# Batches 4 to 7: the first half of the pooled products half a slot sooner, and one P product a slot sooner

## The chip, the cores and the metric

One core of one Trainium2 chip. The metric is the device time of one execution in microseconds (us); the time given for a kernel is the median of its runs. "Profile" and "trace" mean one execution recorded by the hardware profiler.

## The reference

An attention with 32 learned memory slots per head is followed by a two-layer network. For 8 batches, 8 heads, 576 positions and head size 64:

```
a      = softmax(phi)                   # over the 32 memories
k_m    = sum over s of a[s,m] * k[s]    # pooled keys
v_m    = sum over s of a[s,m] * v[s]    # pooled values
attn   = softmax(q @ k_m.T / 8)         # over the 32 memories
x      = attn @ v_m                     # 4608 tokens x 512
h      = x @ w_in                       # 512 x 2048
out    = (h - tanh(h)) @ w_out          # 2048 x 512
```

## The kernel before, in words

**What is computed where.** The tokens are cut into 18 units of 256 tokens, and the 2048 hidden columns into 4 blocks `fb`. Since x is never needed itself, the kernel first makes P = v_m @ w_in for each batch and block (`att_p`, L524, one product per block, called P{b}0 to P{b}3), and then h = attn @ P (`mm1`, L572). All large products run as two or three half-precision products of high and low parts, and h - tanh(h) is a cubic in three VectorE and ScalarE steps. `mm2_blocks` (L686 on; products at L702, L708 and L715) multiplies with w_out in a scheme of seven block products.

**Slots.** After a hand-written start (`START`), one loop runs over slots `sl` from 18 on, one for each unit u and block fb: sl = 4u + fb. In each slot TensorE's own work stands in a fixed order:

- `mm1` of this slot's unit and block, into the one PSUM tile hs; ScalarE squares it (L579) and VectorE goes on with it (L587, L597), ScalarE then rounds it (L603) and GpSimd makes its low part (L608);
- `do(0)`: the first group of this slot's tasks;
- `mm2_blocks` of the unit and block two slots back, into the PSUM tiles x and o;
- `do(1)`: the second group, issued before the rest of the elementwise work;
- after a unit's last block: `evict`, which reads x and o with VectorE (L768 to L780) and sends the result off;
- `do(2)`: the third group, at the slot's end.

**Tasks.** `PLAN` (batches 4 to 7) and `PLAN3` (batch 3) say at which slot, counted from the batch's first one, a task stands. In a string, what is ahead of `;` and `|` goes to `do(0)`, what follows `;` to `do(1)`, what follows `|` to `do(2)`. The first slots of batches 3 to 7 are 24, 36, 44, 52 and 60, so that slot -8 is slot 28, 36, 44 and 52 for batches 4, 5, 6 and 7, and slot -7 is the one after it. `in_order` fixes every engine's instructions in the order in which they are written: nothing is rescheduled, and an instruction that waits holds up all that stands behind it on its engine.

**The tasks the change touches, and their neighbours.**

- KR{b}0, KR{b}1 (`load_kv_half`, L126): keys and values of row half 0 or 1, in two DMAs of 516 KB each (heads 0 and 1, heads 2 and 3), issued by SyncE's queue (SPq). Both halves use the same ring of two buffers (tag "q"), so KR{b}1 can only start when the products on KR{b}0's data are done.
- X, XP, YM, YE (L146, L157, L162 and L168, L182): the softmax of phi. XP brings the maxima to PSUM, ScalarE copies them, GpSimd subtracts them (L162, and L168 twice), ScalarE takes the exponential (L182, tile e). XP and YM are the last tasks of slot -9; YE stands in slot -8, in `do(1)`.
- V{b}0, V{b}1 (`pool_half`, L220, and L228 for the tail): the pooled products of row half 0 or 1, 32 matmuls each with weights from e, and 16 more for the tail in V{b}1. Both write one PSUM tile, pkv. V{b}0 needs the exponential and KR{b}0, V{b}1 needs KR{b}1.
- N, QT, U, S: normalization of the pooled sums, load of q, transposition, scores.
- P{b}3 and PL{b}3 (L524; ScalarE L537; VectorE L542): the last P product of a batch with its two roundings. PSUM tile pp has the same one buffer as pkv and all of the attention's other products.

Of the kernel before, what the change touches and what calls it, by code (L numbers as in the profile page):

```python
# [18 lines left out]
P = 128  # L19
# [318 lines left out]
def split_path(ctx, tc, c, ins, out):  # L338
# [502 lines left out]
    for word in START.split():  # L841
# [5 lines left out]


    PLAN = (
# [5 lines left out]
    PLAN3 = (  # L855
# [3 lines left out]
    )  # L859

    PLAN_C = (
# [227 lines left out]
@with_exitstack  # L1089
def tile_kernel(ctx: ExitStack, tc: tile.TileContext, qt, kva, kvt, pha, phx, w_in, w_out, out):  # L1090
    nc = tc.nc
    ins = dict(qt=qt, kva=kva, kvt=kvt, pha=pha, phx=phx, w_in=w_in, w_out=w_out)
    const = ctx.enter_context(tc.tile_pool(name="const", bufs=1))
    c = {"first": len(nc.cur_bb.bb.instructions)}
    for name, shape, dt in (
        ("ident", [P, P], F32), ("ones", [P, P], F32), ("ones16", [P, 1], F16), ("one", [P, 1], F32),
        ("beta", [P, 1], F32), ("idw", [P, P], F32), ("nidp", [P, P], F16), ("idw", [P, P], F32), ("nid16", [P, P], F16), ("stat", [P, N_CHECK], F32), ("bad", [P, 1], I32),
    ):
        c[name] = const.tile(shape, dt, name=name)
    make_identity(nc, c["ident"])  # L1100
    nc.vector.tensor_scalar(c["nid16"], c["ident"], -1.0, None, op0=ALU.mult)
    nc.vector.tensor_scalar(c["nidp"], c["ident"], -S_V * S_W / S_P, None, op0=ALU.mult)
    nc.vector.tensor_scalar(c["idw"], c["ident"], S_W, None, op0=ALU.mult)
    nc.gpsimd.memset(c["ones"], 1.0)
    nc.gpsimd.memset(c["ones16"], 1.0)
    nc.gpsimd.memset(c["one"], 1.0)
    nc.gpsimd.memset(c["beta"], BETA)
    with ExitStack() as inner:
        split_path(inner, tc, c, ins, out)
    with tc.If(c["wide"] > 0):  # L1110
        with ExitStack() as inner:
            wide_path(inner, tc, c, ins, out)
# [39 lines left out]
```

## Time and profile before

| | |
|---|---|
| median of 3 runs | 660.62 us (660.04 to 660.83) |
| the profiled execution's own time | 660.87 us |
| its span | 659.1 us |
| PE (TensorE matmuls) busy | 641.5 us, 97% |
| DVE (VectorE) busy | 522.7 us, 79% |
| ACT (ScalarE) busy | 375.7 us, 57% |
| POOL (GpSimd) busy | 251.0 us, 38% |
| share of PE in the chain that ended last | 76% |
| TensorE clock granted | full speed over the run |

A timeline row has the start in us, the duration in us, the engine (PEld is TensorE's weight load, SPq is SyncE's queue of DMAs), the line in the kernel, operation, output and inputs, the count, and in brackets the idle time of the engine just before the row and what ended it; "issue" stands for idle time in which nothing that the profile shows was waited for. Rows of one kind that follow each other are merged. The chain view follows back from the last instruction what each piece of work had waited for.

### The profile page before, as it was taken

The page shows a single profiled execution, that of the slowest core. Times are in us where ns is not written, and L with a number is a line of the kernel's source. Part 1 is how long each engine was busy: PE and PEld are TensorE (multiplying, and loading weights), DVE is VectorE, ACT ScalarE, POOL GpSimd, SP SyncE. Part 2 cuts the span into 40 slices and gives each one's busy share as a digit, 9 for nine tenths or more (in the row PEclk, how much of TensorE's full clock was granted, in tenths as well). Part 3 has the DMA queues.
Part 4 walks back from the last instruction along what each step waited for, and adds up shares of the span by engine and source line. Part 5 has one row for each costly group of instructions (what it writes and reads, how often), then busy time and mean ns, then how long its engine had stood idle before and what let it go on. Part 6 is the DMA issues. An engine that isn't in the chain of part 4 may idle for free.

```text
span 659.1 us, 15599 instructions
## 1 busy us (share of the span) xinstructions
PE 641.5 (97%) x6690; PEld 455.5 (69%) x6690; DVE 522.7 (79%) x790; ACT 375.7 (57%) x509; POOL 251.0 (38%) x173
## 2 busy tenths in 40 slices
PE   8879999999999999999999999999999999999996
PEld 4355656566557777777776777777687777887785
DVE  6989999999855787875988679767977686867763
ACT  4567686666424456545655465545654577666541
POOL 0315141221222245442535253625452455455521
PEclk9999999999999999999999999999999999999999
DMA  8999245302423402333331524141505333234201
GB/s 342 375 377 393 96 169 184 114 2 65 145 96 102 145 20 74 113 101 133 105 114 65 168 66 153 60 142 66 163 25 195 101 100 125 61 109 142 77 33 37
DMA packets 25996, 84.98 MB, mean 129 GB/s; under 512 B 2880, under 2 KB 2880, under 8 KB 25152
## 3 DMA queue, kind: packets, MB, share of 16 engines
q1 hardware_dynamic: 24624, 81.55, 36.1%
q10 hardware_dynamic: 1296, 2.36, 0.9%
q8 instruction: 54, 0.88, 0.6%
q14 instruction: 22, 0.18, 0.1%
HBM read 72.37 MB, written 11.53 MB: 127 GB/s over the span
## 4 chain that ended last, share of the span: by engine, by line
PE 76%; DVE 12%; DMA 6%; issue 2%; ACT 2%; POOL 1%; SPq 0%; DVEq 0%; ACTq 0%
PE hs L572 20%; PE x L715 13%; PE o L708 12%; PE o L715 10%; PE o L651 6%; PE h L572 4%; DMA kv<-in_kva_dram 3%; PE o1h L651 3%; PE pp L524 3%; PE pkv L220 2%; DMA raw<-in_w_out_dram 2%; DVE h L587 2%; DVE wt L384 1%; DVE h L597 1%; PE psc L272 1%
## 5 line engine op out<-in xcount | busy, mean ns | idle before, releaser
L608 POOL TENSOR_TENSOR g<-h,g 128x1024 f16<-128x1024 f32 x64 | 138.5, 2165 | 329.2 <-ACT g L603 234.3
L572 PEld LDWEIGHTS <-ph 128*128 128x128 f16 x2304 | 176.7, 98 | 20.7 <-issue 6.0
L572 PE MATMUL hs<-ah,ph 128*128 128x256 f16 (+3 forms) x1152 | 151.5, 246 | 0.0
L587 DVE SCALAR_TENSOR_TENSOR h<-hs,u 128x1024 f32<-128x1024 f32 x54 | 65.9, 1220 | 91.3 <-ACT u L579 91.2
L603 ACT ACTIVATE g<-h 128x1024 f16<-128x1024 f32 x72 | 75.9, 1055 | 91.7 <-DVE h L597 89.5
L572 PE MATMUL hs<-al,ph 128*128 128x256 f16 (+3 forms) x576 | 127.6, 246 | 0.0
L592 ACT ACTIVATE u<-u,beta 128x1024 f32<-128x1024 f32 x72 | 82.4, 1147 | 55.1 <-DVE h L587 54.1
L708 PE MATMUL o<-wout_hi,g 128*128 128x512 f16 x432 | 104.7, 380 | 0.0
L715 PEld LDWEIGHTS <-f 128*128 128x128 f16 x896 | 87.5, 98 | 10.3
L597 DVE SCALAR_TENSOR_TENSOR h<-u,h 128x1024 f32<-128x1024 f32 x72 | 87.4, 1216 | 0.8 <-ACT u L592 0.7
L579 ACT ACTIVATE u<-hs 128x1024 f32<-128x1024 f32 x54 | 55.0, 1019 | 55.3 <-PE hs L572 50.8
L715 PE MATMUL x<-bt,f 128*128 128x256 f16 x672 | 82.5, 273 | 0.0
L715 PEld LDWEIGHTS <-g 128*128 128x128 f16 x672 | 64.1, 98 | 26.6 <-issue 5.0
L708 PEld LDWEIGHTS <-g 128*128 128x128 f16 x432 | 40.5, 98 | 44.0 <-issue 8.1
L651 PEld LDWEIGHTS <-g 128*128 128x128 f16 x384 | 36.6, 98 | 46.6 <-issue 3.4
L621 DVE TENSOR_TENSOR f<-g 128x512 f16<-128x512 f16 x112 | 64.9, 620 | 4.3 <-POOL g L608 3.4
L651 PE MATMUL o<-wout_hi,g 128*128 128x512 f16 x192 | 58.8, 380 | 0.0
L572 PE MATMUL h<-ah,ph 128*128 128x256 f16 (+3 forms) x384 | 49.6, 246 | 0.1
L572 PE MATMUL h<-al,ph 128*128 128x256 f16 (+2 forms) x192 | 42.4, 246 | 0.2 <-POOL al L515 0.2
L542 DVE SCALAR_TENSOR_TENSOR ph<-pp,ph 128x1024 f16<-128x1024 f32 x31 | 37.6, 1213 | 0.6 <-ACT ph L537 0.6
L537 ACT ACTIVATE ph<-pp 128x1024 f16<-128x1024 f32 x32 | 32.5, 1017 | 7.4 <-PE pp L524 7.4
L651 PE MATMUL o<-wout_lo,g 128*128 128x512 f16 x96 | 36.4, 379 | 0.0
(146 smaller groups left out, 979.1 us busy)
## 6 DMA issues: line engine op xcount, KB each, us to landing
kv<-in_kva_dram SPq DMA_DIRECT2D x20, 516.0 KB, 4.2
q<-in_qt_dram SPq DMA_DIRECT2D x16, 576.0 KB, 4.3
chk<-in_w_in_dram SPq DMA_DIRECT2D x16, 512.0 KB, 5.6
chk<-in_w_out_dram SPq DMA_DIRECT2D x16, 512.0 KB, 3.4
out_dram<-r SPq DMA_DIRECT2D x27, 256.0 KB, 2.4
kv<-in_kva_dram SPq DMA_DIRECT2D x6, 1032.0 KB, 9.0
raws<-in_w_in_dram SPq DMA_DIRECT2D x12, 512.0 KB, 7.2
raw<-in_w_out_dram SPq DMA_DIRECT2D x12, 512.0 KB, 6.6
```

Of the source, the lines that this page charges most:

```text
L542: nc.vector.scalar_tensor_tensor(pl, pa, S_P / (S_V * S_W), ph, op0=ALU.mult, op1=ALU.subtract)
L572: nc.tensor.matmul(hp[:, k, tu : tu + w], px[:, g, cs], d[ax][:, g, ta : ta + w], start=(n == 0), stop=(n == 5),)
L579: nc.scalar.activation(uu, hp, AF.Square, scale=1.0 / (S_A * S_P))
L587: nc.vector.scalar_tensor_tensor(h3, hp, C2 * S_G / (S_A * S_P), uu, op0=ALU.mult, op1=ALU.mult)
L592: nc.scalar.activation(uu, uu, AF.Square, bias=c["beta"])
L597: nc.vector.scalar_tensor_tensor(h3, uu, CC, hp, op0=ALU.add, op1=ALU.mult)
L603: nc.scalar.activation(gg[:, 0], h3, AF.Copy)
L608: eng.tensor_tensor(gg[:, 1], h3, gg[:, 0], op=ALU.subtract)
L621: nc.vector.tensor_tensor(o, x, y, op=op)
L651: nc.tensor.matmul(o, gx[:, k, P * tt : P * tt + P], wx[:, 4 * fb + k, :], start=(first and k == 0 and wx is wout_hi and gx is gh), stop=( ...
L708: nc.tensor.matmul(o[th], gg[:, 0, k, P * th : P * th + P], wout_hi[:, 4 * fb + k, :], start=(first and k == 0), stop=False)
L715: nc.tensor.matmul(dst, a(1 - n, kk), b(n, kk), start=(new and kk == 0 and n == 0), stop=(end and kk == 1 and n == 1))
```

## The change

Two tables change, and nothing else. In `PLAN`, V{b}0 goes from the head of slot -7 (`do(0)`, behind `mm1`) to the end of slot -8 (`do(2)`), for batches 4 to 7. KR{b}1 keeps its place at the head of slot -7, where it now is the first task. In `PLAN3`, P33 and PL33 go from slot 26 to slot 25, ahead of batch 3's AE31 and AD31.

```
-  (-8, "; YE{0}"), (-7, "V{0}0 KR{0}1 | V{0}1 N{0} QT{0}0"),
+  (-8, "; YE{0} | V{0}0"), (-7, "KR{0}1 | V{0}1 N{0} QT{0}0"),
...
-  (1, "; AE{0}1 | AD{0}1"), (2, "P{0}3 PL{0}3 ; AT{0}1"),
+  (1, "P{0}3 PL{0}3 ; AE{0}1 | AD{0}1"), (2, "; AT{0}1"),
```

On TensorE, around slots 36 and 37 (batch 5). Names: o and x are tiles of `mm2_blocks`, hs that of `mm1`, pkv that of V50 (weights e, data kv). Before, V50 stands behind the last product of slot 37's `mm1`:

```order
L572 LDWEIGHTS ph_4407
L572 MATMUL hs<-ah_4378,ph_4407 128x256
L220 MATMUL pkv_4603<-kv_4341,e_4166 32x129 [waits DMAHW5_49,DVE_49,Activation_49]
L220 MATMUL pkv_4603<-kv_4341,e_4166 32x129
L220 MATMUL pkv_4603<-kv_4343,e_4166 32x129 [waits DMAHW6_49]
...
L715 LDWEIGHTS g_4453
L715 MATMUL x<-wout_hi,g_4453 128x256
```

Now it stands between the last product of slot 36's `mm2_blocks` and the first of slot 37's `mm1`:

```order
L715 LDWEIGHTS f_4411
L715 MATMUL o_4297<-wout_lo,f_4411 128x256
L220 MATMUL pkv_4575<-kv_4341,e_4166 32x129 [waits DMAHW5_49,DVE_49,Activation_49]
L220 MATMUL pkv_4575<-kv_4341,e_4166 32x129
L220 MATMUL pkv_4575<-kv_4343,e_4166 32x129 [waits DMAHW6_49]
...
L572 LDWEIGHTS ph_4407
L572 MATMUL hs<-ah_4378,ph_4407 128x256
```

V50 has moved ahead of 24 matmuls of `mm1`; its wait for ScalarE (the exponential) has moved with it. SyncE's order is what it was.

On VectorE, slots 25 and 26 (ph is the tile of PL33, f the block forms that `mm2_blocks` uses a slot later, x and o what `evict` reads):

```order
 L587 SCALAR_TENSOR_TENSOR h_3318<-hs,u_3316 128x1024
+L542 SCALAR_TENSOR_TENSOR ph_3345<-pp_3320,ph_3345 128x1024
...
-L780 SCALAR_TENSOR_TENSOR r_3332<-o_2967,r_3332 128x512
...
-L587 SCALAR_TENSOR_TENSOR h_3439<-hs,u_3437 128x1024
-L542 SCALAR_TENSOR_TENSOR ph_3466<-pp_3441,ph_3466 128x1024
...
+L780 SCALAR_TENSOR_TENSOR r_3360<-o_2967,r_3360 128x512
```

PL33 (L542) now stands ahead of slot 25's `evict` instead of behind it; on TensorE the 48 instructions of P33 move from behind slot 26's `mm1` to behind slot 25's.

4 rows, old and new, of tables (PLAN, PLAN3) are left out of this document.

## The prediction

> **What bounds the kernel now.** First the page: the span, and the engine that fills it.
>
> ```profile
> span 659.1 us, 15599 instructions
> PE 641.5 (97%) x6690; PEld 455.5 (69%) x6690; DVE 522.7 (79%) x790; ACT 375.7 (57%) x509; POOL 251.0 (38%) x173
> ```
>
> Since start and end of a span are a case of their own, I next asked for the busy time of the stretch that the slot loop fills (columns: stretch, its length, then busy time and instructions of PE, PEld, DVE, ACT, POOL, then the granted clock, the DMA share and GB/s):
>
> ```profile
> 192.00:606.00 414.00, 411.88 (x4556) 313.00 (x4554) 318.00 (x483) 237.90 (x321) 183.16 (x119) 1.00 0.32 104
> ```
>
> In these 414 us PE is idle for 414.00 - 411.88 = 2.12 us. So PE sets the pace: work on other engines is paid for only where PE has to wait for it, any new wait of PE is paid in full, and no change of order alone can win much more than 2 us here. What little idle time there is, the waits of PE name (total, times, longest, in us), and the chain shows the place; these are its rows around batch 5's V50 and V51:
>
> ```profile
> PE pkv L220 <- DMA kv<-in_kva_dram: 2.5, 3, 1.0
> ```
>
> ```profile
> 351.16 2.62 PE hs L572 x24
> ...
> 355.25 5.54 DMA kv<-in_kva_dram
> 360.79 0.04 issue
> 360.83 1.08 PE pkv L220 x28
> ```
>
> The chain leaves PE for one DMA: V51, the second half of the pooled products, waits for the load KR51. That load had to wait for V50, which frees its buffers. This is the wait that the change can remove. But V50 itself has a supplier, the exponential on ACT, and what matters most below is when that ends. I took the timeline of all four places: for each, the weight loads of `mm1` (their start is where `mm2_blocks` has ended and where V0 will now stand), the exponential L182, V0 and V1. Batch 4, slots 28 and 29:
>
> ```profile
> 283.50 2.61 PEld L572 LDWEIGHTS <-ph 128*128 128x128 f16 x24
> 283.86 1.17 ACT L182 ACTIVATE e<-e 128x1152 f32<-128x1152 f32 x1 [1.30 <-POOL e L168]
> 286.32 0.82 PEld L220 LDWEIGHTS pkv<-kv,e 128*32 128x32 f32 x32 [0.21 <-issue]
> ...
> 292.24 0.97 PEld L220 LDWEIGHTS pkv<-kv,e 128*32 128x32 f32 x32 [0.21 <-issue]
> 293.41 0.18 PEld L228 LDWEIGHTS pkv<-kt,e 64*32 64x32 f32 x16 [0.20 <-issue]
> ```
>
> Batch 5, slots 36 and 37, with the GpSimd work ahead of the exponential:
>
> ```profile
> 347.89 2.36 POOL L162 TENSOR_TENSOR e<-e,ms 128x1024 f32<-128x1024 f32 x1
> 350.20 1.24 POOL L168 TENSOR_TENSOR e<-e,ms 64x128 f32<-64x128 f32 x2
> 350.88 2.61 PEld L572 LDWEIGHTS <-ph 128*128 128x128 f16 x24
> 351.48 1.17 ACT L182 ACTIVATE e<-e 128x1152 f32<-128x1152 f32 x1 [1.85 <-POOL e L168]
> 353.70 0.82 PEld L220 LDWEIGHTS pkv<-kv,e 128*32 128x32 f32 x32 [0.21 <-issue]
> 354.73 0.33 PEld L715 LDWEIGHTS <-g 128*128 128x128 f16 x4 [0.20 <-issue]
> 354.83 0.81 SPq L126 DMA_DIRECT2D kv<-in_kva_dram  x2
> 359.62 0.14 PEld L220 LDWEIGHTS pkv<-kv,e 128*32 128x32 f32 x4 [0.21 <-issue]
> 360.83 0.81 PEld L220 LDWEIGHTS pkv<-kv,e 128*32 128x32 f32 x28 [1.07 <-DMA kv<-in_kva_dram]
> 361.84 0.18 PEld L228 LDWEIGHTS pkv<-kt,e 64*32 64x32 f32 x16 [0.20 <-issue]
> ```
>
> Batch 6, slots 44 and 45:
>
> ```profile
> 420.25 2.72 PEld L572 LDWEIGHTS <-ph 128*128 128x128 f16 x48
> 420.79 1.17 ACT L182 ACTIVATE e<-e 128x1152 f32<-128x1152 f32 x1 [1.79 <-POOL e L168]
> 429.05 0.14 PEld L220 LDWEIGHTS pkv<-kv,e 128*32 128x32 f32 x4 [0.21 <-issue]
> 430.47 0.18 PEld L228 LDWEIGHTS pkv<-kt,e 64*32 64x32 f32 x16 [0.20 <-issue]
> ```
>
> Batch 7, slots 52 and 53:
>
> ```profile
> 489.00 2.77 PEld L572 LDWEIGHTS <-ph 128*128 128x128 f16 x48
> 489.54 1.16 ACT L182 ACTIVATE e<-e 128x1152 f32<-128x1152 f32 x1 [1.79 <-POOL e L168]
> 493.42 1.22 DVE L587 SCALAR_TENSOR_TENSOR h<-hs,u 128x1024 f32<-128x1024 f32 x1 [0.86 <-ACT u L579]
> 497.79 0.14 PEld L220 LDWEIGHTS pkv<-kv,e 128*32 128x32 f32 x4 [0.21 <-issue]
> 498.86 0.81 PEld L220 LDWEIGHTS pkv<-kv,e 128*32 128x32 f32 x28 [0.92 <-DMA kv<-in_kva_dram]
> 499.87 0.18 PEld L228 LDWEIGHTS pkv<-kt,e 64*32 64x32 f32 x16 [0.20 <-issue]
> 500.25 0.84 PEld L572 LDWEIGHTS <-ph 128*128 128x128 f16 x15 [0.20 <-issue]
> ```
>
> In each of the four the exponential starts only after PE has come to the end of slot -8. Today `mm1`, 2.6 to 2.8 us of work, stands between the two and covers it. The change takes that cover away.
>
> **Part 1: the wait that is removed.** Without a wait, V1 takes 293.41 - 292.24 = 1.17 us up to its tail (batch 4). In batches 5, 6 and 7 it takes 361.84 - 359.62 = 2.22, 430.47 - 429.05 = 1.42 and 499.87 - 497.79 = 2.08 us: waits of 1.05, 0.25 and 0.91, together 2.21 us. Do they go? In batch 5 the loads are issued 354.83 - 353.70 = 1.13 us after V50's start, and V51 can go on 360.83 - 353.70 = 7.13 us after it. In the new order, from V50's start to V51's stand V50 (354.73 - 353.70 = 1.03), `mm1` (353.70 - 350.88 = 2.82) and `mm2_blocks` (359.62 - 354.73 = 4.89): 8.74 us. The data is there 1.6 us early, so the whole 2.21 is won. SyncE's queue has the same order as before, so nothing new stands ahead of these loads or is held up behind them for longer. Bounds: 0 won, if the loads take 1.6 + 1.05 us longer, and 2.5 us, the total of the waits view.
>
> **Part 2: the wait that is added.** V0 would start 0.21 us (the issue gap before V0 in batches 4 and 5) after the last weight load of `mm2_blocks`, but the exponential ends later, and 0.04 us (the chain's issue piece between the DMA and V51) go by until PE moves:
>
> - batch 4: 283.86 + 1.17 + 0.04 = 285.07, against 283.50 + 0.21 = 283.71: 1.36 us
> - batch 5: 351.48 + 1.17 + 0.04 = 352.69, against 351.09: 1.60 us
> - batch 6: 420.79 + 1.17 + 0.04 = 422.00, against 420.46: 1.54 us
> - batch 7: 489.54 + 1.16 + 0.04 = 490.74, against 489.21: 1.53 us
>
> Together 6.03 us. What is queued behind V0 on PE is the next slot's `mm1`. Can that run meanwhile? Batch 7 shows it: while V71 waits for its data until 498.86, the `mm1` behind it, whose tile hs is free since VectorE read it (493.42 + 1.22 = 494.64), starts to load weights only at 500.25, after V71. The wait is not filled.
>
> The Trainium skill (TensorE: Matmul & The Clock Gate, Part 2) says why: "The MATMULs themselves stay in program order"; only weight loads are pulled ahead. By that rule this part costs the whole 6.03 us; were matmuls taken out of order it would cost nothing. The trace agrees with the rule.
>
> Nor does the pause bring the exponential forward. It stands behind GpSimd's subtractions, which run without a break from 347.89 to 350.20 + 1.24 = 351.44 in batch 5, 0.04 us before ACT starts; all of it descends from earlier slots that the change leaves alone. Bounds: at the low end the signal costs nothing and the issue gap behind V0 (0.20, as behind V1) is gone, 4 x 0.24 less, 5.1; at the high end the wait brings one more such gap, 4 x 0.20 more, 6.8. I take 6.0, straight from the rows.
>
> The other engines then get slot -7's `mm1` 2.4 to 2.6 us later (the wait and V0), but in the chain rows above they are not on the path, and PE's next use of what they make is a slot or two later.
>
> **Part 3: P33.** PE does the same work, sooner. VectorE gets PL33 ahead of slot 25's `evict`, and slot 26's `mm2_blocks` may write x and o only when `evict` has read them; today P33 stands between. The rows of slot 26 (VectorE's reads L769 and L780, PE's first writes of x and o, PL33):
>
> ```profile
> 261.44 0.42 DVE L769 SCALAR_TENSOR_TENSOR r<-x,r 128x256 f32<-128x256 f32 x1
> 262.45 1.28 DVE L780 SCALAR_TENSOR_TENSOR r<-o,r 128x512 f32<-128x512 f32 x2
> 263.52 0.28 PE L715 MATMUL x<-wout_hi,g 128*128 128x256 f16 x1
> 265.27 1.89 PE L708 MATMUL o<-wout_hi,g 128*128 128x512 f16 x8
> 265.89 1.21 DVE L542 SCALAR_TENSOR_TENSOR ph<-pp,ph 128x1024 f16<-128x1024 f32 x1
> ```
>
> PE writes x and o at the same times as before, since P33 is only exchanged against slot 26's `mm1`. `evict` has done with x at 261.44 + 0.42 = 261.86 and with o at 262.45 + 1.28 = 263.73; it has 263.52 - 261.86 = 1.66 us to spare for x and 265.27 - 263.73 = 1.54 for o, and comes at most 1.21 later. So 0. The margin left is 0.3 us; bounds -0.4 and +0.4.
>
> **The sum.** 6.03 - 2.21 + 0 = +3.82 us on the profiled execution's 660.87 us: 664.69. That execution lies 0.25 above the median of the three runs, so on the median it is 660.62 + 3.82 = 664.4 us, 0.6% slower. About 0.2%, 1.3 us, is the least that a measurement of this kernel can tell from no change.
>
> **Rivals.**
>
> - *The loads stay late.* V0's waits come, V1's stay, because the loads land later or something else holds V1. For it: such a pair was there 292.24 - 286.32 = 5.92 us after V0's start at the latest in batch 4, but only after 7.13 in batch 5, so landings vary by over 1.2 us. Against it: the margin is larger than that, and no wait in four was over 1.05. Price: 660.62 + 6.0 = 666.6. Chance 0.08.
> - *The exponential is in time, and the kernel gets faster.* If ACT's L182 ended 1.4 to 1.6 us sooner against PE, V0 would not wait and only the gain of 2.2 would be left: 658.4 us. It decides at an exponential that starts about 1.0 us ahead of where `mm1`'s weight loads start today. For it: ACT sat idle for 1.30 to 1.85 us before L182, so only GpSimd holds it back. Against it: GpSimd's own row is dense there, and nothing ahead of it changes. Chance 0.04.
> - *The pauses are half given back*, because ACT and VectorE catch up and later slots run tighter: 3.0 - 2.2 = +0.8, 661.4 us, no change that can be told. Against it: PE has 2.12 us idle in 414, and part 1 has used them up. Chance 0.07.
> - *P33 does hold up slot 26*: by its whole 1.21 us, 665.6. Chance 0.02.
>
> That leaves 0.79 for the forecast. The range: from 662.6 (5.1 - 2.5 - 0.4 = +2.2, rounded down) to 666.8 (the first rival's +6.0 with a little of the high bound); left out are the faster case, the half-given-back case and the far end of the dear ones. Faster by over 0.2%: 0.04; within: 0.07; slower: 0.89.
>
> **What would show it.** In the profile of the changed kernel: V0's weight loads with 1.4 to 1.6 us idle "<-ACT e L182" four times; V1's with only the 0.21 of issue; the chain going through GpSimd's e and L182 instead of the DMA of kv; slot 26's first x and o without a wait for VectorE. The prediction is wrong if L220 waits for e under 0.5 us, or if PE's idle time between slots 18 and 60 has not grown by about 4 us.

## The result, and the profile after

| | before | after |
|---|---|---|
| median | 660.98 us (9 runs) | 663.98 us (9 runs) |
| ratio | | 1.0043, 95% interval 1.003 to 1.0057 |
| the profiled execution's own time | 660.87 us | 664.19 us |
| its span | 659.1 us | 662.4 us |

The change makes the kernel slower, by 0.43% or 2.8 us (2.0 to 3.8). The forecast was +3.8 us. The page and the stretch of the slot loop, as for the kernel before:

```profile
span 662.4 us, 15598 instructions
PE 640.7 (97%) x6690; PEld 455.5 (69%) x6690; DVE 518.5 (78%) x790; ACT 376.2 (57%) x509; POOL 251.2 (38%) x173
```

```profile
192.00:606.00 414.00, 407.76 (x4535) 310.65 (x4534) 311.01 (x480) 236.69 (x318) 179.75 (x117) 1.00 0.32 105
```

In the same 414 us PE is now idle for 414.00 - 407.76 = 6.24 us instead of 2.12, 4.1 us more. That is more than the kernel lost. From the start of slot 18 to the start of slot 60, the same piece of the program in both traces, PE's idle time is again 2.12 and 6.24 us, but the piece is only 362.28 - 359.23 = 3.05 us longer. So idle time is a sign and not the account: a part of a wait can count as busy time, as V1's old waits will show. PE's waits say what it waits for:

```profile
PE pkv L220 <- ACT e L182: 5.6, 4, 1.6
...
PE pkv L220 <- DMA kv<-in_kva_dram: 0.6, 1, 0.6
```

The wait for the loads, 2.5 us before, has gone but for one in the start, and four waits for the exponential have come. In the chain around batch 5 the DMA is replaced by ACT:

```profile
350.25 2.47 DVE f L621 x3
352.71 0.02 issue
352.74 1.17 ACT e L182
353.91 0.04 issue
353.95 1.09 PE pkv L220 x32
355.04 2.73 PE hs L572 x24
```

The chain puts VectorE's f ahead of L182, because it ended last; the waits of ACT name GpSimd's L168 there, as before. Next come the weight loads of V0, of V1 and of V1's tail in batches 4, 5, 6 and 7, and for batch 5 also the exponential:

```profile
285.09 0.82 PEld L220 LDWEIGHTS pkv<-kv,e 128*32 128x32 f32 x32 [1.31 <-ACT e L182]
293.63 0.82 PEld L220 LDWEIGHTS pkv<-kv,e 128*32 128x32 f32 x32 [0.21 <-issue]
294.65 0.18 PEld L228 LDWEIGHTS pkv<-kt,e 64*32 64x32 f32 x16 [0.20 <-issue]
...
352.74 1.16 ACT L182 ACTIVATE e<-e 128x1152 f32<-128x1152 f32 x1 [1.86 <-POOL e L168]
353.95 0.82 PEld L220 LDWEIGHTS pkv<-kv,e 128*32 128x32 f32 x32 [1.83 <-ACT e L182]
362.48 0.82 PEld L220 LDWEIGHTS pkv<-kv,e 128*32 128x32 f32 x32 [0.21 <-issue]
363.50 0.18 PEld L228 LDWEIGHTS pkv<-kt,e 64*32 64x32 f32 x16 [0.20 <-issue]
...
423.68 0.82 PEld L220 LDWEIGHTS pkv<-kv,e 128*32 128x32 f32 x32 [1.77 <-ACT e L182]
432.28 0.82 PEld L220 LDWEIGHTS pkv<-kv,e 128*32 128x32 f32 x32 [0.21 <-issue]
433.30 0.18 PEld L228 LDWEIGHTS pkv<-kt,e 64*32 64x32 f32 x16 [0.20 <-issue]
...
493.61 0.82 PEld L220 LDWEIGHTS pkv<-kv,e 128*32 128x32 f32 x32 [1.78 <-ACT e L182]
502.20 0.82 PEld L220 LDWEIGHTS pkv<-kv,e 128*32 128x32 f32 x32 [0.21 <-issue]
503.22 0.18 PEld L228 LDWEIGHTS pkv<-kt,e 64*32 64x32 f32 x16 [0.20 <-issue]
```

Less the 0.21 us of issue that V0 had anyway, V0 waits 1.10, 1.62, 1.56 and 1.57 us: 5.85. V1 up to its tail takes 1.02 us in all four batches (for example 294.65 - 293.63). Against that the four of before, 1.17, 2.22, 1.42 and 2.08, held waits of 0.15, 1.20, 0.40 and 1.06 us: 2.81. So the account is 5.85 - 2.81 = +3.04. Of the 2.81 us, only 1.45 had shown as idle time of PE (all that the kernel before has between the starts of slots 28 and 55); of V0's 5.85, it is 5.57.

It can be checked without any of these rows, by the start of `mm1`'s weight loads in a slot, in both traces:

| slot | before | after | later by | more than the line above |
|---|---|---|---|---|
| 28 | 275.99 | 276.29 | 0.30 | |
| 30 (after V1 of batch 4) | 293.79 | 295.03 | 1.24 | 0.94 |
| 38 (batch 5) | 362.22 | 363.88 | 1.66 | 0.42 |
| 46 (batch 6) | 430.85 | 433.68 | 2.83 | 1.17 |
| 54 (batch 7) | 500.25 | 503.60 | 3.35 | 0.52 |
| 71 (the last) | 636.59 | 639.94 | 3.35 | 0.00 |

The four places give 3.05 us, and nothing is given back between them or behind them. (Slots 26, 29, 37, 45 and 53 can't be compared in this way, because P33 or V0 has moved past the start of their `mm1`.) The first 0.30 us stand there at slot 18 already, ahead of the change: they are a difference of two executions in the start.

### The profile page after: what moved, and what is told of

Read it like the earlier page. It is cut to its first block, busy times and chain, and to the rows that moved or that the text cites. A ratio compares the mean times of both kernels' runs of the same rounds, so it can differ in the third digit from the quotient of the medians.

```text
span 662.4 us, 15598 instructions
## 1 busy us (share of the span) xinstructions
PE 640.7 (97%) x6690; PEld 455.5 (69%) x6690; DVE 518.5 (78%) x790; ACT 376.2 (57%) x509; POOL 251.2 (38%) x173
## 4 chain that ended last, share of the span: by engine, by line
PE 76%; DVE 14%; ACT 3%; DMA 2%; issue 2%; POOL 1%; ACTq 0%; DVEq 0%; POOLq 0%
PE hs L572 20%; PE x L715 13%; PE o L708 12%; PE o L715 9%; PE o L651 6%; PE h L572 4%; PE o1h L651 3%; PE pp L524 3%; DVE f L621 3%; DMA raw<-in_w_out_dram 2%; DVE h L587 2%; PE pkv L220 2%; PE warm L789 2%; DVE wt L384 1%; DVE h L597 1%
## 5 line engine op out<-in xcount | busy, mean ns | idle before, releaser
L603 ACT ACTIVATE g<-h 128x1024 f16<-128x1024 f32 x72 | 75.9, 1056 | 87.7 <-DVE h L597 85.5
L597 DVE SCALAR_TENSOR_TENSOR h<-u,h 128x1024 f32<-128x1024 f32 x72 | 87.4, 1217 | 0.8 <-ACT u L592 0.7
L621 DVE TENSOR_TENSOR f<-g 128x512 f16<-128x512 f16 x112 | 61.5, 590 | 3.7 <-POOL g L608 3.4
L542 DVE SCALAR_TENSOR_TENSOR ph<-pp,ph 128x1024 f16<-128x1024 f32 x31 | 37.6, 1214 | 0.6 <-ACT ph L537 0.6
```

The source lines that it names most:

```text
L542: nc.vector.scalar_tensor_tensor(pl, pa, S_P / (S_V * S_W), ph, op0=ALU.mult, op1=ALU.subtract)
L597: nc.vector.scalar_tensor_tensor(h3, uu, CC, hp, op0=ALU.add, op1=ALU.mult)
L603: nc.scalar.activation(gg[:, 0], h3, AF.Copy)
L621: nc.vector.tensor_tensor(o, x, y, op=op)
```

## The experiments

The theory: V0 waits for the exponential, V1 no longer for its loads, and P33's place is worth nothing. Each time is compared with the kernel before on the same chip, whose median was between 660.56 and 660.96 us.

**Each part alone.** V0 moved as in the change, P33 left in slot 26:

```
   PLAN:   (-8, "; YE{0} | V{0}0"), (-7, "KR{0}1 | V{0}1 N{0} QT{0}0")
   PLAN3:  (1, "; AE{0}1 | AD{0}1"), (2, "P{0}3 PL{0}3 ; AT{0}1")
```

> V0 moved for batches 4 to 7, P33 left in slot 26. Stall theory: TensorE waits for the exponential at V0 in all four batches (1.1 to 1.6 us each, 6.1 us together, batch 4's at 1.36 instead of the 1.10 of the full change), V1's waits are gone, +3.3 us on the kernel before, 664.3 us. Rival (P33 makes the time): without P33's move the time falls back by over 1 us, to 662.9 or less. Rival (P33 hides some of the wait): batch 4's wait at V0 grows by about 0.3 us and nothing else changes; this is within the stall theory's numbers and shows only in the trace.

Measured: 664.14 us, ratio 1.0046 (1.003 to 1.0062); by slot starts the four batches give +3.24 us. V0 alone makes the whole loss. And P33 moved alone:

```
   PLAN:   (-8, "; YE{0}"), (-7, "V{0}0 KR{0}1 | V{0}1 N{0} QT{0}0")
   PLAN3:  (1, "P{0}3 PL{0}3 ; AE{0}1 | AD{0}1"), (2, "; AT{0}1")
```

> P33 moved to slot 25, V0 left where it was. Stall theory: no wait is added or removed, 0 +- 0.4 us, 661.0 us; V0 without a wait, V1's waits as before. Rival (P33 makes the time): +1 us or more, with a wait of TensorE for VectorE's reads of x or o in slot 26.

Measured: 660.68 us, ratio 0.9995 (0.9983 to 1.0008): no difference. But P33 does touch V0's wait. In the run with V0 alone, batch 4's V0 reads

```profile
284.87 0.82 PEld L220 LDWEIGHTS pkv<-kv,e 128*32 128x32 f32 x32 [1.57 <-ACT e L182]
```

that is 1.57 - 0.21 = 1.36 us, exactly the prediction's term, where the full change has 1.10. PL33's 1.2 us less on VectorE in slot 26 let batch 4's elementwise chain, and with it the exponential, come 0.26 us sooner against PE. The two traces show the way: in slot 27 ScalarE's rounding L603 waits for VectorE's L597, and the copy of the maxima, which GpSimd's subtraction and the exponential follow, stands behind L603. L597 begins 0.47 us ahead of slot 28's `mm1` in the full change and only 0.20 us with V0 alone.

**Take V0's wait away.** V0 only reads row half 0 of e. GpSimd's subtraction and ScalarE's exponential are cut by row half, half 0 first (shortened):

```
   for r in range(2):
       v = e[:, 0:8].rearrange("p (c r) x -> p c r x", r=2)[:, :, r]
       gpsimd.tensor_tensor(v, v, <maxima of half r>, op=subtract)
   ...
   for v in (<half 0>, <half 1>, e[:, 8]):
       scalar.activation(v, v, Exp)
```

> The full change, and for batches 4 to 7 the subtraction (GpSimd) and the exponential (ScalarE) cut by row half, half 0 first, which is all that V0 reads. Stall theory: the exponential of half 0 ends over 1 us ahead of the end of slot -8, V0 waits for nothing but the issue gap, V1's waits stay away, so 2.8 us faster than the kernel before: 658.2 us. Rival (the place itself costs: single-precision products between the two half-precision streams break the stream whatever they wait for): no faster than 661, V0's idle time is gone but the slots around it stay longer. Rival (another input is late too, such as the load of half 0): V0 goes on waiting, for a DMA, 662 to 664 us.

Measured: 658.85 us, ratio 0.997 (0.9954 to 0.9986), that is -2.0 us against the kernel before, -3.0 to -0.9. Batch 5 (GpSimd's two halves, the first exponential, V0, V1 and its tail; the old lines' numbers are 13 higher, and L182 is now the new loop of subtractions):

```profile
347.49 2.69 POOL L182 TENSOR_TENSOR e<-e,ms 128x512 f32<-128x512 f32 x2
...
349.14 0.61 ACT L195 ACTIVATE e<-e 128x512 f32<-128x512 f32 x1
...
350.69 0.82 PEld L233 LDWEIGHTS pkv<-kv,e 128*32 128x32 f32 x32 [0.21 <-issue]
...
359.22 0.82 PEld L233 LDWEIGHTS pkv<-kv,e 128*32 128x32 f32 x32 [0.21 <-issue]
360.25 0.18 PEld L241 LDWEIGHTS pkv<-kt,e 64*32 64x32 f32 x16 [0.20 <-issue]
```

The exponential of half 0 ends at 349.75, V0 starts at 350.69 with the issue gap alone, and V1 waits for nothing. By slot starts the four batches give -0.15, -1.20, -0.39 and -1.05 us, together -2.8: V1's waits of before, one by one, and no price for V0's new place.

The same cut in the kernel before, V0 behind `mm1`:

> The kernel before, with the subtraction and the exponential cut by row half as in the row split, V0 and P33 where they were. Stall theory: V0 never waited there, since the next slot's first product covers the exponential, so a sooner exponential wins nothing: 0 +- 0.4 us, 661.0 us; V1 waits for its loads as before. Rival (the split is what wins, by freeing GpSimd or ScalarE): as fast as the row split with the change.

Measured: 661.21 us, ratio 1.0005 (0.9991 to 1.0018). So the cut wins nothing by itself; it wins where V0 stands ahead of `mm1`. With the cut and V0 moved, but P33 left in slot 26:

> The row split with V0 moved and P33 left in slot 26. Stall theory: once V0 waits for nothing, P33's place is worth nothing: 658.2 us, as with P33 moved, to 0.4 us. Rival (P33 helps by taking VectorE's backlog out of slots 26 and 27): 0.5 us or more slower than the row split with P33 moved.

Measured: 658.22 us, ratio 0.9963 (0.995 to 0.9977), as good as with P33 moved, and by slot starts -2.8 us again: its place is worth nothing. These two versions beat the kernel before by 2 us or more.

**Half a dose.** Only the exponential is cut, eight full blocks first and the tail block after:

```
   for v in (e[:, 0:8], e[:, 8]):
       scalar.activation(v, v, Exp)
```

> The full change, and for batches 4 to 7 only the exponential cut in two: the eight full blocks first, which need only the long subtraction, then the tail block, which V0 does not read. Stall theory: the exponential that V0 waits for starts about 1.2 us sooner and takes 1.05 us, so V0 waits 0 to 0.4 us a batch, 0.8 us together in place of 5.9: 659.0 us, between the row split and the kernel before. Rival (the place itself costs): 662 or more.

Measured: 659.85 us, ratio 0.9986 (0.9972 to 0.9999), so -0.9 us, -1.9 to -0.1: less than the -2.0 that was expected. In the trace the four batches do give it: by slot starts -0.15, -0.89, -0.13 and -0.80, together -2.0. Part of the difference lies outside the profiled spans: the time of a run exceeds its span by 2.4 us here and by 1.8 us in the kernel before (medians), and no run shows why. Batch 5's V0 still waits 0.52 - 0.21 = 0.31 us (line numbers are 4 higher):

```profile
351.62 0.82 PEld L224 LDWEIGHTS pkv<-kv,e 128*32 128x32 f32 x32 [0.52 <-ACT e L186]
```

**More of the wait.** One more pass of ScalarE over e (a copy onto itself) ahead of the exponential, first in the kernel before, then behind the change:

```
   scalar.activation(e, e, Copy)
   scalar.activation(e, e, Exp)
```

> The kernel before with the same extra pass of ScalarE. Stall theory: the 2.6 to 2.8 us of the next slot's first product cover all but the last 0.1 to 0.3 us a batch, so +0.2 to +1.0 us: 661.2 to 662.0 us, against +4.6 us for the same delay behind the change. Rival (ScalarE itself is near the bound): as much as behind the change, over 664.

Measured: 661.99 us, ratio 1.0021 (1.0008 to 1.0034), +1.4 us, 0.5 to 2.2, where +0.2 to +1.0 was expected. In the trace slot 54 starts 0.46 us later against slot 18, and this comes at batch 5: V0 waits 0.20 us there, and V1 0.27 us longer than before for its load. In the other three batches V0 waits 0.04 us at most, so `mm1` covers almost the whole delay. Why the runs lose more than this one execution is not shown.

> The full change, and for batches 4 to 7 one more pass of ScalarE over e (a copy onto itself, 1.17 us or a little less) ahead of the exponential. Stall theory: the wait at V0 grows by the whole of it in all four batches, 4 x 1.15 = +4.6 us on the changed kernel: 668.6 us, 1.2% over the kernel before. Rival (pauses are given back by the other engines, or the place itself costs and not the wait): 666 or less.

Measured: 673.07 us, ratio 1.0178 (1.0161 to 1.0196): +9.4 us on the changed kernel when slot starts are compared from slot 18 on, where +4.6 was expected. (The profiled execution, 676.64 us, was the slowest of the six: 3.2 us of it stand there at slot 18 already.) The direction holds, the size does not. Batches 4 and 5 (V0 and the `mm1` behind it; line numbers are 2 higher, and the view names no releaser here, but in each batch V0 starts 0.07 us after the exponential's end):

```profile
289.24 0.85 PEld L222 LDWEIGHTS pkv<-kv,e 128*32 128x32 f32 x32 [2.53 <-issue]
290.29 2.52 PEld L574 LDWEIGHTS <-ph 128*128 128x128 f16 x24 [0.20 <-issue]
...
359.32 0.85 PEld L222 LDWEIGHTS pkv<-kv,e 128*32 128x32 f32 x32 [3.04 <-issue]
360.38 4.18 PEld L574 LDWEIGHTS <-ph 128*128 128x128 f16 x24 [0.20 <-issue]
```

The waits are 2.53 - 0.21 = 2.32, 2.83, and in batches 6 and 7 2.77 and 2.76 us: 10.68, or 4.83 over the change's 5.85, as the theory has it. The rest, 4.6 us, lies in the products behind the wait: batch 5's `mm1` takes 4.18 us instead of 2.52. The stretches of 4 us behind the start of V0 in the four batches show why (the third number from the right is the granted clock):

```profile
290.00:294.00 4.00, 4.00 (x49) 3.43 (x39) 0.00 (x0) 0.99 (x2) 2.12 (x1) 1.00 0.58 165
360.20:364.20 4.00, 4.00 (x31) 2.79 (x21) 0.00 (x0) 0.00 (x1) 3.24 (x2) 0.57 0.61 211
433.00:437.00 4.00, 4.00 (x60) 3.53 (x51) 0.00 (x0) 0.00 (x0) 3.21 (x2) 0.66 0.52 170
505.50:509.50 4.00, 4.00 (x70) 3.62 (x63) 0.00 (x0) 0.07 (x1) 3.24 (x2) 0.76 0.38 124
```

Behind three of the four waits the granted clock fell. Two smaller doses were to tell whether the clock is the whole rest, a copy of three and of six of the nine blocks:

```
   scalar.activation(e[:, 6:9], e[:, 6:9], Copy)     # or e[:, 3:9]
   scalar.activation(e, e, Exp)
```

> The full change with a small delay: for batches 4 to 7 ScalarE copies three of the nine blocks of e onto themselves (128x384, about 0.5 us) ahead of the exponential. Theory (the wait is paid one to one, and only a pause of some 2.7 us or more also takes the clock down for a few us): waits of 1.6 to 2.1 us at V0, granted clock 1.00 there, 4 x 0.5 = +2.0 us on the changed kernel. Rival (what the whole extra pass cost above its length comes with any delay, in proportion): twice that, +4 us.

> The full change with a middle delay: six of nine blocks copied (128x768, about 0.85 us) ahead of the exponential. Theory: waits of 1.9 to 2.5 us at V0, +3.4 us on the changed kernel as long as the granted clock stays at 1.00 there; wherever it falls to one half in the 4 us behind V0, 1.3 to 1.7 us more for that batch, and for no other. Rival (in proportion to the delay): +6.9 us with the clock at 1.00.

Measured: 670.06 us, ratio 1.013 (1.0099 to 1.0161), and 671.17 us, ratio 1.0163 (1.0132 to 1.0194). The totals of the profiled executions, +3.95 and +6.87 us on the changed kernel by slot starts, are the rival's numbers; the batches are not. The +2.0 us expected for three blocks was missed in any case: a drop of the clock was expected only behind pauses of some 2.7 us or more. For three blocks, the stretches behind V0 and two of the waits, batch 5 and batch 6:

```profile
285.40:289.40 4.00, 4.00 (x46) 3.44 (x36) 0.00 (x0) 1.26 (x2) 2.12 (x1) 1.00 0.60 183
354.80:358.80 4.00, 4.00 (x47) 3.41 (x38) 0.36 (x2) 1.26 (x2) 3.24 (x2) 1.00 0.59 191
425.00:429.00 4.00, 4.00 (x61) 3.55 (x54) 0.45 (x3) 0.43 (x1) 3.24 (x2) 0.64 0.38 129
497.20:501.20 4.00, 4.00 (x70) 3.69 (x62) 0.36 (x2) 1.20 (x2) 3.24 (x2) 1.00 0.58 208
```

```profile
353.96 0.85 PEld L222 LDWEIGHTS pkv<-kv,e 128*32 128x32 f32 x32 [2.39 <-issue]
...
424.28 1.40 PEld L222 LDWEIGHTS pkv<-kv,e 128*32 128x32 f32 x32 [2.34 <-issue]
426.07 3.48 PEld L574 LDWEIGHTS <-ph 128*128 128x128 f16 x48 [0.39 <-issue]
```

The two pauses are alike, 2.18 and 2.13 us, and only behind the second V0 and `mm1` are slower: 1.40 against 0.82 and 3.48 against 2.63 us in the changed kernel, with the gap between them 0.19 longer, 1.62 us in all. The waits have grown by 2.25 us and the one drop of the clock costs 1.62, together 3.87 of the 3.95. For six blocks the waits, 9.39 us in all, have grown by 3.54, and two drops (batches 4 and 7, stretches at 0.57 and 0.71) cost 1.66 and 1.58: 6.78 of the 6.87. The wait is paid one to one; what comes on top is the clock. The medians lie above these two profiled executions, some 6.5 and 7.6 us over the changed kernel (9.5 and 10.6 over the kernel before, less the change's 3.0). For three blocks the other four runs have mean granted clocks of 0.990 to 0.993 against the profiled one's 0.996, which fits more drops; for six blocks this is so in two of four (0.988 against 0.993), and what made the other two 1 us slower stays open.

Why does one pause take the clock down, and another of the same length not? In these traces the granted clock changes only at marks 3.41 us apart. The three drops of the whole extra pass begin at 360.64, 432.32 and 504.00 us, which is 21 steps of 3.413 us each time; the two drops of six blocks, at 286.27 and 497.89, are 62 such steps apart; and each of the six drops lasted one step, at a clock of 0.50. Here are the waits of batches 5 and 7 with six blocks, 2.50 and 2.44 us long; for each, the step that holds most of the wait, and the step behind it:

```profile
354.53:357.94 3.41, 1.47 (x36) 1.26 (x37) 2.72 (x6) 2.76 (x3) 0.49 (x1) 1.00 0.00 0
357.95:361.36 3.41, 3.41 (x34) 3.06 (x32) 0.00 (x0) 1.02 (x1) 2.74 (x2) 1.00 0.72 243
494.48:497.89 3.41, 1.04 (x10) 0.69 (x7) 3.38 (x6) 2.07 (x3) 1.20 (x3) 1.00 0.00 0
497.89:501.30 3.41, 3.38 (x47) 3.02 (x48) 0.85 (x3) 0.88 (x1) 2.40 (x2) 0.50 0.12 23
```

The longer wait straddles a mark and leaves PE idle for 3.41 - 1.47 = 1.94 us of its step; the shorter one fills 3.41 - 1.04 = 2.37 us, and only behind it does the clock fall. The same for all sixteen waits (where no drop shows a mark, the marks are counted in steps of 3.413 us from where the trace first has the clock at full speed):

| run | PE idle in the step, batches 4, 5, 6, 7 | of these, followed by a drop |
|---|---|---|
| the change | 1.03, 1.55, 1.49, 1.43 | none |
| three blocks | 1.63, 1.17, 2.09, 1.86 | 2.09 |
| six blocks | 1.96, 1.94, 1.50, 2.37 | 1.96 and 2.37 |
| the whole pass | 1.96, 2.12, 2.73, 2.00 | 2.12, 2.73 and 2.00 |

Every step with 2.00 us or more of idle time was followed by a drop, and none with 1.94 us or less. The border is not that sharp: of the two steps with 1.96 us only one was followed by a drop, and in the start of two other runs a drop followed steps with 1.85 and 1.93 us. This order was found in the traces afterwards; no run was made to test it.

## Why the prediction was right, and where its sizes were off

- **What bounds.** That PE sets the pace held. The bound of 2.12 us to win did not: the best versions win 2.0 and 2.4 us in the runs, but 2.8 by slot starts. From slot 18 to slot 60 the row split still has 0.67 us of PE idle time, so only 1.45 of its 2.8 us came out of idle time. The other half had counted as busy, as in batch 4 before, where V1 has no gap in its row and still takes 0.15 us too long.
- **Part 1, the wait removed.** The mechanism held: V1 waits for nothing in any batch. The size, 2.21 us, was too small. The step that failed is "Without a wait, V1 takes 1.17 us (batch 4)": batch 4 had a wait too, short enough not to be named in its rows. Unhindered V1 takes 1.02 us, so 2.81 us were won, 0.60 more, and more than the 2.5 us that the prediction gave as the most. The yardstick was taken from one of the places that were to be measured with it.
- **Part 2, the wait added.** 6.03 us forecast, 5.85 measured. Three of the four terms are within 0.04 us (1.60, 1.54, 1.53 against 1.62, 1.56, 1.57). Batch 4's, 1.36, came out as 1.10, and the run without P33's move gives 1.36. PE did not fill the wait with the `mm1` behind it.
- **Part 3, P33.** 0 on its own: held. What was overlooked is that VectorE's backlog of slot 26 reaches batch 4's exponential, and that taking PL33 out of it saves 0.26 us of the new wait. That "all of it descends from earlier slots that the change leaves alone" was wrong for batch 4.
- **The sum.** +3.82 forecast, +3.04 in the trace, +2.8 (2.0 to 3.8) in the runs; the terms that were off were 0.60 and 0.26 us, both towards less. The sign that PE's idle time would grow by about 4 us came true (4.12 us) partly by luck: it was meant to follow the +3.8 us, but idle time grew by more than the kernel lost.
- **The rivals.** The loads did not stay late: in the trace they have landed 2.38 to 2.58 us before V1 starts, more than the 1.6 us that was forecast. The exponential was not in time, but the row split shows that rival's kernel, at 658.2 to 658.9 us for a forecast of 658.4. The pauses were not given back: between the four places no slot start that can be compared moved by more than 0.01 us. P33 held up nothing in slot 26. Here are its rows after (VectorE's reads, PE's first writes of x and o):

```profile
262.12 0.42 DVE L769 SCALAR_TENSOR_TENSOR r<-x,r 128x256 f32<-128x256 f32 x1
...
263.13 1.28 DVE L780 SCALAR_TENSOR_TENSOR r<-o,r 128x512 f32<-128x512 f32 x2
```

```profile
263.82 0.27 PE L715 MATMUL x<-wout_hi,g 128*128 128x256 f16 x1
...
265.57 1.89 PE L708 MATMUL o<-wout_hi,g 128*128 128x512 f16 x8
```

`evict` has done with x at 262.54 and with o at 264.41 and so has 1.28 and 1.16 us to spare: it came 0.4 us closer, not the 1.21 that was allowed for, since f's pair no longer ran beside GpSimd and took 0.75 us instead of 1.50.

## What to carry to other kernels

Before a product is moved ahead so that a load behind it can start, look at when its other inputs are ready: the work that it is moved past may be what covers them, and where the matmuls run in order, as TensorE's did in every trace here, the uncovered time is paid in full, and a wait of 2 us or more may, as here, cost some clock on top. The cheap repair was to cut the producer, so that the part the product reads comes first. And take the time of an unhindered instruction from a place that cannot have waited, the shortest of all, and not from the one beside the waits; idle time alone does not show every wait.

## What the runs showed of the hardware that was not expected

A pause of TensorE can cost more than its length, and which pause does depends on where it falls. The granted clock changed only at marks 3.41 us apart, whose place differed from execution to execution. Behind a step between two marks in which TensorE was idle for 2.00 us or more it was 0.50 for the whole next step, in all five such cases among the sixteen waits; behind 1.94 us or less, in none of nine. Length alone does not sort them: a pause of 2.50 us left the clock at 1.00, one of 2.01 us did not. A step at half the clock can cost at most 3.41 / 2 = 1.71 us; the six drops cost 1.3 to 1.7 us, least behind the one wait in which the step began well before V0 did (by 0.69 us).

The Trainium skill (TensorE: Matmul & The Clock Gate, Part 1) describes a gate that halves the clock after an idle window of about 3.4 us, and a window that runs freely. The half clock, the step of 3.41 us and marks that lie elsewhere in each execution agree with that; that the window has to be idle throughout does not: about 2.0 of the 3.41 us were enough here.

VectorE's half-precision pair L621 took 2.21 us in slot 36 of the kernel before, where GpSimd's subtraction L162 began 1.03 us ahead of it and ran on beside it (and L168 behind L162):

```profile
347.89 2.36 POOL L162 TENSOR_TENSOR e<-e,ms 128x1024 f32<-128x1024 f32 x1
348.92 2.21 DVE L621 TENSOR_TENSOR f<-g 128x512 f16<-128x512 f16 x2
```

In slot 26, where GpSimd had nothing, the same pair took 0.75 us:

```profile
267.02 0.75 DVE L621 TENSOR_TENSOR f<-g 128x512 f16<-128x512 f16 x2
```

In the kernel before, from 190 us on, none of the 177 instructions of L621 that ran with GpSimd idle took more than 0.43 us; beside GpSimd single ones took up to 1.63 us. No run here shows what that costs the kernel, but an elementwise time from one slot is not that of another.
